# The first load of a decode kernel, cut into eight transfers of 16 rows

## The chip, the cores and the metric

The kernel runs on one core of one Trainium2 chip. Times are device microseconds (us) of that core. Executions of one kernel agree within about 0.3% (six of the kernel before: 353.45 to 353.86 us). A profile is one such execution with the hardware profiler on; its span is some 2 us shorter than the timed figure, so spans are compared with spans and times with times.

## The reference

One new token passes through two branches, mixed by a scalar gate. Branch A is attention with 32 query heads over 8 cached key/value heads of 32,768 positions; branch B is a small gated feed-forward layer. Everything is bf16. The code is shortened.

```python
def _A_ref(x, k_cache, v_cache, wq, wo):           # x [1,1,512], wq [512, 4096]
    q = (x @ wq).reshape(B, Sq, Hq, Dh).transpose(0, 2, 1, 3)
    ...
    scores = jnp.einsum("bhqd,bhkd->bhqk", q, k) * (Dh ** -0.5)
    p = _softmax(scores, axis=-1)
    o = jnp.einsum("bhqk,bhkd->bhqd", p, v)        # k, v: [1, 8, 32768, 128] each
    return o.transpose(0, 2, 1, 3).reshape(B, Sq, Hq * Dh) @ wo

def _B_ref(x, w_gate, w_up, w_down):
    return (_silu(x @ w_gate) * (x @ w_up)) @ w_down

g = _sigmoid((x * gate_w).sum(-1, keepdims=True))
return g * a + (1 - g) * b
```

The two caches are 128 MiB together and every byte is read once. The arithmetic is small; the bytes are the work.

## The kernel before

All loads are issued by the SyncE queue, in one fixed order, into a ring of five slots of 32 KB per partition. Each slot is 128 partitions (rows) high. wq comes first. The code is shortened; its comments are ours.

```python
stream = [("wq",), ("K", 0, 0), ("F1",), ("K", 0, 1), ("F2",)]     # F1: w_gate, w_up; F2: w_down
for g in range(1, G):
    for hf in range(2):
        stream += [("K", g, hf), ("V", g - 1, hf)]
stream += [("V", G - 1, 0), ("V", G - 1, 1), ("wo",)]
...
wq_v = slot_of(("wq",)).rearrange("p (c n) -> p c n", c=KC)        # 128 rows, 32 KB each
...
@block.sync
def _(sp):
    for i, e in enumerate(stream):
        ld = sem_ld[place[e]]
        if e in before:
            sp.wait_ge(*released[before[e]])       # the slot's last reader
        if e[0] == "wq":
            sp.dma_start(wq_v, A_wq.rearrange("(p c) n -> p c n", c=KC)).then_inc(ld, 16)
        ...
        elif e[0] == "F2":
            sp.dma_start(wd, B_w_down.rearrange("(p j) n -> p j n", j=FC)).then_inc(ld, 16)
...
def emit_q():                                      # TensorE
    take(load_sem(("wq",)), 16)
    for h in range(H):
        for c in range(KC):
            ins = pe.matmul(...)                   # q = x @ wq
```

Partition p of the slot gets rows 4p to 4p+3 of wq, which are 32 KB in one piece in memory. In the trace wq's 128 rows are 128 packets of 32 KB, and wq's semaphore gets sixteen updates, from 12.51 to 13.31 us. We read this as sixteen DMA engines with eight rows each, every one of which adds one to the semaphore when its share has landed, hence the wait for 16.

Of the kernel before, what the change touches and what calls it, by code (L numbers as in the profile page):

```python
# [13 lines left out]
def bass_gated_mix__gqa_block_cached__swiglu_ffn__decode_kernel(  # L14
# [23 lines left out]
    KC = D // 128  # L38
# [21 lines left out]
    NSC = 2  # L60
    NET = 2
    SCALE = float(DH) ** -0.5
    WO_CUT = (16, 8, 4, 4)
    assert NI * PB == 32 and sum(WO_CUT) == WOJ

# [19 lines left out]
    with ExitStack() as es:  # L85

        def S_(name):
            return es.enter_context(nc.semaphore(name))
# [5 lines left out]
        sem_ldv = S_("s_ldv")  # L94
        sem_ldo = [S_(f"s_ldo{i}") for i in range(len(WO_CUT))]
        sem_x = S_("s_x")
# [130 lines left out]
        def slot_of(entry):  # L227
            return ring[:, place[entry], :]

        def kv_slot(entry):  # L230
            return slot_of(entry).rearrange("p (r d) -> p r d", r=RH)

        wq_v = slot_of(("wq",)).rearrange("p (c n) -> p c n", c=KC)
# [12 lines left out]
        def load_sem(entry):  # L246
            return sem_ld[place[entry]]

        with nc.Block("main") as block:
# [60 lines left out]
# [4 lines that stand above are left out]
                    if e in before:  # L314
                        sp.wait_ge(*released[before[e]])
                    if e[0] == "wq":
                        sp.dma_start(wq_v, A_wq.rearrange("(p c) n -> p c n", c=KC)).then_inc(
                            ld, 16
                        )
                    elif e[0] == "F1":  # L320
                        sp.dma_start(wg, B_w_gate.rearrange("(p c) f -> p c f", c=KC)).then_inc(
                            ld, 16
                        )
                        sp.dma_start(wu, B_w_up.rearrange("(p c) f -> p c f", c=KC)).then_inc(
                            ld, 16
                        )
                    elif e[0] == "F2":
                        sp.dma_start(wd, B_w_down.rearrange("(p j) n -> p j n", j=FC)).then_inc(
                            ld, 16
                        )  # L330
                    elif e[0] == "wo":
                        src = A_wo.rearrange("(p j) n -> p j n", j=WOJ)
                        j0 = 0
                        for c, n in enumerate(WO_CUT):
                            sp.dma_start(wo_v[:, j0 : j0 + n, :], src[:, j0 : j0 + n, :]).then_inc(  # L335
                                sem_ldo[c], 16
                            )
                            j0 += n
                    else:
                        kind, g, hf = e  # L340
                        src = (A_k_cache if kind == "K" else A_v_cache)[
                            0, g, hf * (S // 2) : (hf + 1) * (S // 2), :
                        ].rearrange("(p r) d -> p r d", r=RH)
                        dst = kv_slot(e)
                        if e == ("V", G - 1, 1):
                            sp.dma_start(dst[:, : RH // 2, :], src[:, : RH // 2, :]).then_inc(  # L346
                                ld, 16
                            )
                            sp.dma_start(dst[:, RH // 2 :, :], src[:, RH // 2 :, :]).then_inc(  # L349
                                sem_ldv, 16  # L350
                            )
                        else:
                            sp.dma_start(dst, src).then_inc(ld, 16)  # L353
                sp.wait_ge(sem_res, 1)
                sp.dma_start(
                    out[0, 0, :].rearrange("(c n) -> c n", c=OC), res[0:128:32, :]
                ).then_inc(sem_out, 16)
                sp.wait_ge(sem_out, 16)

            @block.tensor  # L360
            def _(pe):
                def take(sem, n):
                    pe.wait_ge(sem, n)
                    pe.sem_inc(sem, -n)  # L364
# [19 lines left out]
                    ).then_inc(sem_pe_g, 1)  # L384

                def emit_q():
                    take(load_sem(("wq",)), 16)
                    for h in range(H):
                        for c in range(KC):
                            ins = pe.matmul(  # L390
                                ps_m[:, M_Q0 + h : M_Q0 + h + 1],
                                wq_v[:, c, h * DH : (h + 1) * DH],
                                xT[:, c : c + 1],
                                start=(c == 0),
                                stop=(c == KC - 1),
                            )
                    ins.then_inc(sem_pe_q, 1)
                    pe.wait_ge(sem_sel, 2)
                    pe.wait_ge(sem_qT, 1)
                    for e in range(2):  # L400
                        ins = pe.matmul(
                            ps_m[:, M_QE + e * H : M_QE + (e + 1) * H],
                            sel[:, e, :],
                            qT[:, :],
                            start=True,
                            stop=True,
                        )
                    ins.then_inc(sem_pe_qe, 1)
# [127 lines left out]
                pe.wait_ge(sem_ident, 2)  # L536
                pe.wait_ge(sem_osel, 1)
                emit_q()
                emit_k(0, first=True)
                emit_ffn()  # L540
# [33 lines left out]
                j0 = 0  # L574
                for c, n in enumerate(WO_CUT):
                    pe.wait_ge(sem_ldo[c], 16)
# [13 lines left out]
            def _(act):  # L590
# [15 lines left out]
                for g in range(G):  # L606
# [3 lines left out]
                    for hf in range(2):  # L610
                        f = 2 * g + hf
                        if f >= 2:
# [5 lines left out]
                            bias=nbias[:, 0:1],  # L618
                            scale=SCALE,
                            accum_out=esum[:, g, hf : hf + 1],  # L620
# [8 lines left out]
            def _(dve):  # L629
# [101 lines left out]
                def emit_k(hf, each):  # L731
# [10 lines left out]
                    if hf == 0:  # L742
# [12 lines left out]
                        dve.scalar_tensor_tensor(  # L755
                            gsel[:, :], gmax[:, :], -SCALE, mask4[:, :], ALU.mult, ALU.mult
                        ),
# [99 lines left out]
```

## Time and profile before

| | before |
|---|---|
| time, median of 3 (range) | 353.69 us (353.55 to 353.71) |
| span of the profiled run | 351.6 us |
| bytes read | 148.11 MB |
| load queue's packets, share of 16 engines' span | 98.3% |
| TensorE busy / VectorE busy | 72% / 56% |

The page's data-rate line has the GB/s moved in each of 40 equal slices of the span. The line of the load queue (q1) has its packets, its MB and the share of sixteen engines' span that the packets took.

```profile
GB/s 325 436 406 438 421 440 439 429 427 429 431 432 436 429 429 432 440 425 429 432 440 425 432 429 440 429 429 429 440 432 425 432 436 432 429 429 436 414 418 184
...
q1 hardware_dynamic: 5912, 148.12, 98.3%
```

From the second slice to the last but one, the rate stays within 406 to 440. The engines are full from end to end, and the first and last slices are the only thin ones.

The table of stretches has, for each stretch, its length, the busy time (and instruction count) of TensorE, weight loads, VectorE, ScalarE and GpSimd, then TensorE's granted clock, the DMA engines' share and the GB/s. A packet is counted whole in the stretch in which it starts, so short stretches are rough and a share can exceed 1.

```profile
core 0: us, PE busy (x) PEld busy (x) DVE busy (x) ACT busy (x) POOL busy (x), PEclk, DMA share, GB/s
4.00:12.00 8.00, 1.00 (x10) 0.83 (x10) 0.55 (x4) 0.17 (x1) 0.00 (x0) 1.00 0.97 410
12.00:20.00 8.00, 3.11 (x117) 3.14 (x118) 2.23 (x12) 0.00 (x0) 2.02 (x7) 1.00 1.03 442
20.00:28.00 8.00, 4.30 (x36) 4.17 (x34) 3.72 (x12) 0.30 (x1) 0.00 (x0) 1.00 0.96 401
28.00:36.00 8.00, 7.74 (x73) 5.35 (x71) 7.51 (x13) 0.00 (x0) 0.00 (x0) 1.00 1.04 449
...
44.00:100.00 56.00, 43.75 (x450) 32.49 (x449) 38.55 (x71) 5.01 (x13) 0.76 (x2) 0.90 1.01 433
```

410 GB/s while wq lands, and 433 later.

SyncE's timeline (start, duration, instruction) shows when the loads are issued:

```profile
0.73 0.38 SPq L317 DMA_DIRECT2D ring<-in_A_wq_dram  x1
1.18 0.41 SPq L353 DMA_DIRECT2D ring<-in_A_k_cache_dram  x1
...
37.12 0.33 SPq L353 DMA_DIRECT2D ring<-in_A_k_cache_dram  x1
```

One issue for wq at 0.73 us, taking 0.38 us. The six first issues are done by 3.7 us; the next waits for a free slot until 37.12 us.

TensorE's timeline has the two places where it takes up the early loads (line 390 multiplies with wq, line 446 transposes the first K). In brackets stand the idle time before and what ended it:

```profile
16.89 3.55 PE L390 MATMUL ps<-xT,ring 128*128 128x1 bf16 x128 [6.67 <-PEq L364]
...
24.36 4.58 PE L446 MATMUL ps<-ident_f,ring 128*128 128x128 f32 x24 [2.74 <-PEq L364]
```

The end of the chain of waits, in order of time (start, duration, what):

```profile
308.15 38.86 DMA ring<-in_A_wo_dram
...
349.19 0.35 DVE res L821
```

The chain hangs on the last wo transfer. From its landing (348.19 us by the semaphore records) to the end of the span are 3.4 us.

Behind these views stand the packet records of the trace file. The lines below are worked out from them and are no view of the profile. Taken sixteen at a time in order of start, the 32 KB packets (one row of wq, then of K) of the first loads read:

```
before  row 1   start 1.77 to 2.77, mean  1.98   took 1.25 to 2.11, mean 1.887   mean end  3.87
before  row 2   start 3.64 to 4.16, mean  3.87   took 1.22 to 1.24, mean 1.237   mean end  5.10
before  row 5   start 7.28 to 8.14, mean  7.59   took 1.21 to 1.70, mean 1.271   mean end  8.86
before  row 8   start 10.91 to 11.76, mean 11.29  took 1.21 to 1.23, mean 1.214   mean end 12.50
before  row 9   start 12.12 to 12.98, mean 12.50  took 1.21 to 1.21, mean 1.213   mean end 13.71
```

Rows 1 to 8 are wq, row 9 the first row of K on each engine. A row takes 1.213 us on one engine: 32,768 B / 1.213 us = 27.0 GB/s, times sixteen 432 GB/s.

### The profile page before, as it was taken

How to read it: one execution, taken by the hardware profiler on the slowest of the kernel's cores; microseconds unless marked ns; L12 is line 12 of the kernel's file. 1: busy time of each engine (PE TensorE's matmuls, PEld its weight loads, DVE VectorE, ACT ScalarE, POOL GpSimd, SP SyncE). 2: the span in 40 equal slices, each digit the busy share in tenths (PEclk: the TensorE clock that was granted, in tenths of full speed). 3: DMA queues.
4: the chain of work that ended last, by engine and by line, in shares of the span. 5: the costliest groups of instructions: out<-in, count | busy, mean ns of one | idle time of the engine just before them, and what ended most of it. 6: DMA issues, size and time to landing. Idle time of an engine off the chain costs nothing. (4 is left out here: it accounts for less than half of the span.)

```text
span 351.6 us, 6018 instructions
## 1 busy us (share of the span) xinstructions
PE 252.5 (72%) x2623; PEld 184.6 (53%) x2623; DVE 196.8 (56%) x367; ACT 17.6 (5%) x52; POOL 5.6 (2%) x22
## 2 busy tenths in 40 slices
PE   0159896978395957858495968768497929688755
PEld 0157884745282626546383838455474618475423
DVE  1329276958184845838283756648365917558211
ACT  1000001100100010000100010000100010000100
POOL 0200000000000000000000000000000000000000
PEclk9999679999789998989789698989779987969665
DMA  8999999999999999999999999999999999999994
GB/s 325 436 406 438 421 440 439 429 427 429 431 432 436 429 429 432 440 425 429 432 440 425 432 429 440 429 429 429 440 432 425 432 436 432 429 429 436 414 418 184
DMA packets 5924, 148.24 MB, mean 422 GB/s; under 512 B 666, under 2 KB 668, under 8 KB 924
## 3 DMA queue, kind: packets, MB, share of 16 engines
q1 hardware_dynamic: 5912, 148.12, 98.3%
q8 instruction: 7, 0.11, 0.1%
q14 instruction: 1, 0.01, 0.0%
q10 hardware_dynamic: 4, 0.00, 0.0%
HBM read 148.11 MB, written 0.00 MB: 421 GB/s over the span
## 5 line engine op out<-in xcount | busy, mean ns | idle before, releaser
L736 DVE COPY ktT<-ps 128x1024 bf16<-128x1024 bf16 x256 | 163.3, 685 | 95.5 <-PE ps L446 92.9
L446 PE MATMUL ps<-ident_f,ring 128*128 128x128 f32 x1024 | 158.2, 311 | 56.0 <-PEq L364 56.0
L446 PEld LDWEIGHTS ps<-ident_f,ring 128*128 128x128 f32 x1024 | 133.8, 161 | 89.8 <-issue 65.6
L460 PE MATMUL ps<-ktT,qc 128*32 128x512 bf16 x512 | 41.6, 402 | 15.2 <-DVE ktT L736 15.1
L510 PE MATMUL ps<-ring,ET 128*16 128x512 bf16 x512 | 33.6, 407 | 2.9 <-DMA ring<-in_A_v_cache_dram 2.9
L510 PEld LDWEIGHTS ps<-ring,ET 128*16 128x16 bf16 x512 | 13.3, 92 | 19.3 <-DMA ring<-in_A_v_cache_dram 3.8
L460 PEld LDWEIGHTS ps<-ktT,qc 128*32 128x32 bf16 x512 | 7.9, 95 | 28.1 <-DVE ktT L736 24.3
L741 DVE TENSOR_REDUCE pmaxf<-ps 128x1 f32<-128x512 f32 x16 | 11.1, 692 | 13.7 <-DVEq L740 13.7
L525 PEld LDWEIGHTS ps<-osel,pv_sb 128*128 128x128 f32 x72 | 11.6, 244 | 3.0 <-issue 3.0
L525 PE MATMUL ps<-osel,pv_sb 128*128 128x4 f32 x72 | 11.3, 281 | 1.8 <-PEq L364 1.8
L598 ACT ACTIVATE qc<-qz 128x112 bf16<-128x112 bf16 x8 | 2.4, 296 | 198.6 <-DVE nbias L759 186.5
L614 ACT ACTIVATE P<-ps,nbias 128x512 bf16<-128x512 f32 x16 | 10.7, 675 | 30.2 <-DVE nbias L759 30.1
L772 DVE COPY pv_sb<-ps 128x512 f32<-128x512 f32 x9 | 6.1, 682 | 6.1 <-PE ps L510 6.1
L390 PE MATMUL ps<-xT,ring 128*128 128x1 bf16 x128 | 3.6, 165 | 6.7 <-PEq L364 6.7
L306 POOL PARTITION_ALL_REDUCE gmax<-pmax x8 | 3.0, 372 | 307.4 <-DVE pmax L748 307.4
L492 PE MATMUL ps<-ident,P 128*128 128x128 bf16 x64 | 6.2, 219 | 1.9 <-ACT P L614 1.4
L766 DVE COPY ET<-ps 128x512 bf16<-128x512 bf16 x16 | 6.7, 416 | 1.3 <-PE ps L492 1.3
L415 PEld LDWEIGHTS ps<-xT,ring 128*128 128x128 bf16 x112 | 6.8, 159 | 0.4 <-issue 0.4
L390 PEld LDWEIGHTS ps<-xT,ring 128*128 128x128 bf16 x128 | 3.5, 104 | 6.7 <-issue 6.7
L415 PE MATMUL ps<-xT,ring 128*128 128x1 bf16 x112 | 6.9, 198 | 0.0
L373 PE MATMUL ps<-ones_bf,x_row 1*128 1x1 bf16 x4 | 0.3, 171 | 8.5 <-DMA gw_row<-in_gate_w_dram 8.5
L492 PEld LDWEIGHTS ps<-ident,P 128*128 128x128 bf16 x64 | 4.8, 98 | 2.8 <-ACT P L614 1.9
(71 smaller groups left out, 36.9 us busy)
## 6 DMA issues: line engine op xcount, KB each, us to landing
ring<-in_A_k_cache_dram SPq DMA_DIRECT2D x16, 4096.0 KB, 24.9
ring<-in_A_v_cache_dram SPq DMA_DIRECT2D x15, 4096.0 KB, 32.5
ring<-in_A_wq_dram SPq DMA_DIRECT2D x1, 4096.0 KB, 12.6
ring<-in_A_v_cache_dram SPq DMA_DIRECT2D x2, 2048.0 KB, 29.4
ring<-in_A_wo_dram SPq DMA_DIRECT2D x1, 2048.0 KB, 36.0
ring<-in_B_w_gate_dram SPq DMA_DIRECT2D x1, 1792.0 KB, 26.7
ring<-in_B_w_up_dram SPq DMA_DIRECT2D x1, 1792.0 KB, 30.6
ring<-in_B_w_down_dram SPq DMA_DIRECT2D x1, 1792.0 KB, 43.5
```

Of the source, the lines that this page charges most:

```text
L390: ins = pe.matmul(ps_m[:, M_Q0 + h : M_Q0 + h + 1], wq_v[:, c, h * DH : (h + 1) * DH], xT[:, c : c + 1], start=(c == 0), stop=(c == KC - 1),)
L415: ins = pe.matmul(ps_m[:, base + j : base + j + 1], wt[:, c, :].rearrange("d (p j) -> d j p", j=FC)[:, j, :], xT[:, c : c + 1], start=(c = ...
L446: ins = pe.transpose(stb[:, t * 64 : (t + 2) * 64], two.bitcast(FP32), ident_f[:, :])
L460: ins = pe.matmul(ps_sc[hf][32 * c : 32 * c + 32, :], qc[:, e, 24 - PB * i : 56 - PB * i], kt[:, e, :], start=(i == 0 and e == 0), stop=(i ...
L492: ins = pe.transpose(ps_pt[:, hf * 512 + m * 128 : hf * 512 + (m + 1) * 128], P[:, hf, m * 128 : (m + 1) * 128], ident[:, :],)
L510: ins = pe.matmul(ps_pv[32 * c : 32 * c + 2 * PB, :], ET[:, hf, col : col + 2 * PB], src[:, i0 : i0 + 2, c, 2 * m : 2 * m + 2, :].rearrang ...
L525: ins = pe.matmul(ps_m[:, M_OT : M_OT + HPG], pv_sb[:, r * DH : (r + 1) * DH], osel[:, r * HPG : (r + 1) * HPG], start=(r == 0), stop=(r = ...
L614: act.activation(P[:, hf, :], ps_sc[hf], ACT.Exp, bias=nbias[:, 0:1], scale=SCALE, accum_out=esum[:, g, hf : hf + 1],).then_inc(sem_exp, 1)
L736: dve.tensor_copy(ktT[:, q % NKT, :], pst[q % NST]).then_inc(sem_cp, 1)
L741: ins = dve.tensor_reduce(pmaxf[:, hf : hf + 1], ps_sc[hf], AX.X, ALU.max)
L766: dve.tensor_copy(ET[:, hf, :], ps_pt[:, hf * 512 : (hf + 1) * 512]).then_inc(sem_ptc, 1)
L772: dve.tensor_copy(pv_sb[:, :], ps_pv).then_inc(sem_pvc, 1)
```

## The change: intent and diff

The intent is a faster start. The sixteen first packets start over a whole microsecond (1.77 to 2.77 us). If the first transfer held only one row for each engine, each might get its first row sooner. Rows r, r+8, r+16 and so on go in transfer r.

```diff
+    WQ_CUT = 8
...
                     if e[0] == "wq":
-                        sp.dma_start(wq_v, A_wq.rearrange("(p c) n -> p c n", c=KC)).then_inc(
-                            ld, 16
-                        )
+                        src = A_wq.rearrange("(p c) n -> p c n", c=KC)
+                        for r in range(WQ_CUT):
+                            sp.dma_start(wq_v[r::WQ_CUT, :, :], src[r::WQ_CUT, :, :]).then_inc(
+                                ld, 16
+                            )
...
                 def emit_q():
-                    take(load_sem(("wq",)), 16)
+                    take(load_sem(("wq",)), 16 * WQ_CUT)
```

Same bytes, same 32 KB packets, same place in SBUF; seven more issues. No engine's order of instructions changes otherwise (line numbers move by three).

## The prediction

> **What bounds the kernel now.** The page's part 3 puts the load queue's packets at 98.3% of 16 engines' span: 148.12 MB in 351.6 us. In the packet records a 32 KB packet (one row of wq, K or V) takes 1.213 us on one engine, 27.0 GB/s, 432 for sixteen, with no gaps between packets; the table of stretches reads 431 to 433 GB/s from 30 to 300 us. PE is 72% busy, VectorE 56%. The chain of waits ends in the last wo transfer (11%) and a tail of 3 us after its landing at 348.2 us. So the time is: first packet (1.77 us), byte stream, tail. What lengthens the stream adds in full; compute that starts later costs nothing while it keeps ahead.
>
> **The start.** SyncE issues wq at 0.73 us. The sixteen first packets start between 1.77 and 2.77 us (twelve by 2.01) and take 1.7 to 2.1 us (the last 1.25). wq lands engine by engine from 12.51 to 13.31 us. TensorE takes it up at 16.86 us, since it waits for constants (GpSimd restarts at 12.4 us).
>
> **What the change removes and adds.**
> - Intended gain: each engine gets its first row at once. At best the last start moves from 2.77 to about 2.0 us: 0.8 us.
> - Issues: seven more on SyncE, about 0.47 us each with gaps, 3.3 us. They stay ahead of the engines (a row takes 1.21 us), and the loads behind them are not needed until wq is through. About 0.
> - Packets: the same; seven more completion writes per engine[...].
> - **The partitions written at once.** This decides. [...]
>
> **On the critical path.** All of it, as the stream has no slack: +9.7 us, less up to 0.8 us of start: +8.9 to +9.7. Everything later shifts with it: PE's q work (3.6 us) starts at about 22 us rather than 16.9, still ahead of the first K load (24.2 us, then about 33).
>
> **Predicted time: 362.6 us (+2.5%)**, range 353.0 to 364.0. Two humps: about two thirds at 361.5 to 363.5, a quarter at 353 to 354[...], the rest between (engines fall out of step). Chances: faster by over 2%: 0.01; within 2%: 0.32; slower by over 2%: 0.67.
>
> **What would show it.** Table of stretches, 4 to 12 us: about 216 GB/s in place of 410; first 32 KB packets 2.4 us; wq landing at about 22 us after eight issues; K's first landing at about 33 us; from 35 us on the same 432 GB/s; the same tail. Right on the start: first packets all within about 0.3 us.
>
> **What would make it wrong.** [...] Then the time stays at 353 to 358.

The sum was +9.7 us (each of the eight wq rows of an engine 1.213 us longer, 2.43 us in all), less up to 0.8 us at the start: +8.9 to +9.7 us. The 362.6 us predicted are 353.7 + 8.9. That a row would double was not shown when this was written.

## The result, and the profile after

| | before | after |
|---|---|---|
| time, median of 6 (range) | 353.62 us (353.45 to 353.86) | 364.05 us (363.80 to 364.33) |
| span of the profiled run | 351.6 us | 362.0 us |
| ratio | 1 | 1.0295 (95%: 1.0282 to 1.0308) |

The change made the kernel slower by 10.4 us, 2.95%. The prediction had said slower by 8.9 us, with a range that ends 0.05 us below the measured median.

The data rate by slices and the load queue after the change:

```profile
GB/s 174 232 290 419 448 407 433 455 409 440 422 442 427 431 438 420 449 413 453 413 438 427 442 427 427 442 420 449 413 438 424 442 427 435 435 427 442 413 412 188
...
q1 hardware_dynamic: 6024, 148.12, 98.3%
```

The three first slices fell from 325, 436 and 406 to 174, 232 and 290 GB/s; the rest is as it was. The queue's engines are still "98.3% busy": a packet that takes 2.55 us in place of 1.21 counts as busy for all of it. The share of busy engines does not see this loss; the rate does.

The table of stretches after (same columns):

```profile
4.00:12.00 8.00, 1.01 (x10) 0.84 (x10) 0.55 (x4) 0.17 (x1) 0.16 (x1) 1.00 1.00 205
12.00:20.00 8.00, 0.00 (x0) 0.00 (x0) 2.22 (x12) 0.00 (x0) 1.86 (x7) 1.00 1.21 250
20.00:28.00 8.00, 3.55 (x128) 3.50 (x128) 0.62 (x4) 0.00 (x0) 0.00 (x0) 1.00 0.84 332
28.00:36.00 8.00, 1.65 (x9) 1.60 (x10) 1.34 (x8) 0.30 (x1) 0.00 (x0) 1.00 0.93 396
...
44.00:100.00 56.00, 48.42 (x564) 35.93 (x562) 38.43 (x69) 3.38 (x8) 0.62 (x2) 0.91 1.00 429
```

205 GB/s in place of 410 while wq lands: half. From 44 us on, 429 against 433.

SyncE's timeline:

```profile
0.74 5.01 SPq L320 DMA_DIRECT2D ring<-in_A_wq_dram  x8
5.79 0.58 SPq L356 DMA_DIRECT2D ring<-in_A_k_cache_dram  x1
...
47.32 0.33 SPq L356 DMA_DIRECT2D ring<-in_A_k_cache_dram  x1
```

The eight issues take 5.01 us, 0.63 us each. The next load is issued at 5.79 us. Its data is not needed until 22 us, so the queue itself is not the cause. The issue that waits for a slot moved from 37.12 to 47.32 us, by 10.2 us.

TensorE:

```profile
23.75 3.55 PE L393 MATMUL ps<-xT,ring 128*128 128x1 bf16 x128 [16.49 <-PEq L367]
...
34.57 4.57 PE L449 MATMUL ps<-ident_f,ring 128*128 128x128 f32 x24 [6.09 <-PEq L367]
```

TensorE now does wait for wq (idle for 16.5 us before line 393), but it is through with q at 28.5 us and still waits for K until 34.57 us. That moved by 10.2 us too.

The end of the chain of waits:

```profile
318.37 38.86 DMA ring<-in_A_wo_dram
...
359.56 0.35 DVE res L824
```

The same end, 10.2 to 10.4 us later.

The packet records, again sixteen at a time:

```
after   row 1   start 2.11 to 2.83, mean  2.29   took 1.81 to 2.72, mean 2.293   mean end  4.58
after   row 2   start 4.12 to 4.95, mean  4.59   took 2.53 to 2.55, mean 2.542   mean end  7.13
after   row 5   start 11.75 to 12.59, mean 12.24  took 2.39 to 2.40, mean 2.388   mean end 14.62
after   row 8   start 19.25 to 20.09, mean 19.73  took 2.54 to 2.55, mean 2.549   mean end 22.28
after   row 9   start 21.80 to 22.64, mean 22.28  took 1.46 to 1.90, mean 1.641   mean end 23.92
after   row 10  start 23.69 to 24.09, mean 23.92  took 1.21 to 1.23, mean 1.219   mean end 25.14
```

Rows 2 to 8 take 2.39 to 2.55 us in place of about 1.21, on all sixteen engines. The first K row (row 9) takes 1.64 us, and from row 10 on it is 1.22 us again. Row 5, the one with r = 4, is the short one, with 2.39 us. Where the 10 us come from, by mean ends: the start 0.31 us later (1.98 to 2.29), row 1 longer by 0.41, rows 2 to 8 by 9.07 (17.70 against 8.63), row 9 by 0.43; together 10.2. Nothing of it is given back: the mean landing of the first K moved by 10.24 us (22.76 to 33.00), that of the last wo transfer by 10.25 (347.27 to 357.52).

### The profile page after: what moved, and what is told of

The parts are those of the page before. It is cut to its first block, busy times and chain, and to the rows that moved or that the text cites. A ratio compares the mean times of both kernels' runs of the same rounds, so it can differ in the third digit from the quotient of the medians.

```text
span 362.0 us, 6025 instructions
## 1 busy us (share of the span) xinstructions
PE 252.3 (70%) x2623; PEld 184.6 (51%) x2623; DVE 196.6 (54%) x367; ACT 17.6 (5%) x52; POOL 5.6 (2%) x22
## 3 DMA queue, kind: packets, MB, share of 16 engines
q1 hardware_dynamic: 6024, 148.12, 98.3%
## 5 line engine op out<-in xcount | busy, mean ns | idle before, releaser
L393 PE MATMUL ps<-xT,ring 128*128 128x1 bf16 x128 | 3.6, 165 | 16.5 <-PEq L367 16.5
L393 PEld LDWEIGHTS ps<-xT,ring 128*128 128x128 bf16 x128 | 3.5, 104 | 16.5 <-issue 16.5
```

What stands on the lines that cost most here:

```text
L393: ins = pe.matmul(ps_m[:, M_Q0 + h : M_Q0 + h + 1], wq_v[:, c, h * DH : (h + 1) * DH], xT[:, c : c + 1], start=(c == 0), stop=(c == KC - 1),)
```

## The experiments

Three theories were set against each other.

- **T1, the partitions.** How long a row takes depends on which SBUF partitions a transfer writes.
- **T2, colliding reads.** Sixteen engines read wq at a pitch of 256 KB at the same moment, and collide in memory.
- **T3, a cost per transfer.** Every transfer ends with a completion on each engine (so we read the load queue's rise from 5,912 to 6,024 packets, by 7 × 16 of 4 B); if the next row waited for it, eight transfers at 1.33 us extra (2.55 − 1.21) would give the same 10.6 us.

All three fit the result. Diffs below are against the changed kernel, unless noted. Each run was timed in three rounds beside the kernel before, on the same chip. E1 to E4, E5 to E8 and E9 to E10 shared chips; "before" measured 353.77, 353.66 and 353.85 us there.

| run | wq goes as | row 2 took | time | ratio (95%) |
|---|---|---|---|---|
| before | 1 × 128 rows | 1.24 us | 353.62 | 1 |
| after | 8 × 16, step 8 | 2.54 us | 364.05 | 1.0295 (1.0282 to 1.0308) |
| E1 | 8 × 16, step 8; reads consecutive | 2.55 us | 363.54 | 1.0278 (1.0261 to 1.0295) |
| E2 | 8 × 16 consecutive | 4.61 us | 379.84 | 1.0738 (1.0720 to 1.0756) |
| E3 | 8 × 128 rows, an eighth of the columns | (4 KB packets) | 354.00 | 1.0001 (0.9984 to 1.0018) |
| E4 | 1 × 128; w_down as 8 × 16, step 8 | 1.23 us | 359.13 | 1.0146 (1.0129 to 1.0163) |
| E5 | 7 × 16, step 7, then 16 consecutive | 2.13 us | 363.09 | 1.0268 (1.0251 to 1.0285) |
| E6 | 4 × 32, step 4 | 1.24 us | 353.73 | 1.0006 (0.9989 to 1.0023) |
| E7 | 2 × 64, step 2 | 1.24 us | 353.80 | 1.0005 (0.9988 to 1.0022) |
| E8 | as after | 2.53 us | 363.73 | 1.0282 (1.0265 to 1.0299) |
| E9 | 4 × 32 consecutive | 2.56 us | 363.61 | 1.0279 (1.0262 to 1.0296) |
| E10 | 2 × 64 consecutive | 2.54 us | 363.84 | 1.0288 (1.0270 to 1.0305) |

"Row 2 took" is the mean of the second sixteen 32 KB packets.

### E1: the writes as in the change, the reads consecutive

```diff
-                            sp.dma_start(wq_v[r::WQ_CUT, :, :], src[r::WQ_CUT, :, :]).then_inc(
-                                ld, 16
-                            )
+                            sp.dma_start(
+                                wq_v[r::WQ_CUT, :, :], src[16 * r : 16 * r + 16, :, :]
+                            ).then_inc(ld, 16)
```

> Eight transfers of 16 rows into every eighth partition, as in the change, but each read from 16 consecutive rows of wq (wrong result on purpose). T1[...], so rows of about 2.55 us, wq through at about 22.3 us, time 353.6 + 10.4 = 364 (362.5 to 365). T2, the reads at a pitch of 256 KB collide in HBM: pitch is now 32 KB, rows back to about 1.21 us, time 353 to 355. T3, each transfer's completion holds its engine up by about 1.3 us: eight transfers as before, 364.

The rows of wq land in the wrong partitions, on purpose. (The check of the result passed all the same, so it says nothing about the order of these rows.) Measured: 363.54 us, rows of 2.55 us. The table of stretches:

```profile
4.00:12.00 8.00, 1.01 (x10) 0.84 (x10) 0.55 (x4) 0.17 (x1) 0.69 (x3) 1.00 1.10 225
12.00:20.00 8.00, 0.00 (x0) 0.00 (x0) 2.23 (x12) 0.00 (x0) 1.34 (x5) 1.00 1.13 234
```

225 GB/s against 205 after the change in this stretch (and 234 against 250 in the next): the same rate over both. T2 falls: it is not the order of the reads. (The ratio is 1.0278 against 1.0295; the intervals overlap, and a small part for the reads can be neither claimed nor excluded.)

### E2: sixteen consecutive rows

```diff
-                            sp.dma_start(wq_v[r::WQ_CUT, :, :], src[r::WQ_CUT, :, :]).then_inc(
-                                ld, 16
-                            )
+                            sp.dma_start(
+                                wq_v[16 * r : 16 * r + 16, :, :], src[16 * r : 16 * r + 16, :, :]
+                            ).then_inc(ld, 16)
```

> Eight transfers of 16 consecutive rows into 16 consecutive partitions (right result). T1: [...]first rows 4.9 to 5.1 us, later rows between 2.5 and 5 us[...]; wq through between 33 and 42 us, time +20 to +29, 374 to 383. T2: source pitch 32 KB, so 353 to 355. T3: still eight transfers, 364.

Measured: 379.84 us, +26.1. The table of stretches:

```profile
4.00:12.00 8.00, 1.00 (x10) 0.84 (x10) 0.55 (x4) 0.17 (x1) 0.83 (x4) 1.00 1.16 131
```

131 GB/s with eight transfers as before, and reads as plain as they can be. T3 and T2 had 364 and 354. Rows 2 to 8 all take 4.60 to 4.64 us, 3.8 times the 1.213 us of the kernel before. They did not become shorter, as the expectation had allowed for (2.5 to 5 us); the engines stay in step. (The 131 GB/s of the stretch are rough at 4.6 us a packet; the packet records give 16 × 32,768 B / 4.62 us = 113.5 GB/s.)

### E3: eight transfers, all partitions

```diff
-                            sp.dma_start(wq_v[r::WQ_CUT, :, :], src[r::WQ_CUT, :, :]).then_inc(
-                                ld, 16
-                            )
+                            c, n = r // 2, r % 2 * 2048
+                            sp.dma_start(
+                                wq_v[:, c, n : n + 2048], src[:, c, n : n + 2048]
+                            ).then_inc(ld, 16)
```

> Eight transfers of all 128 partitions and an eighth of the columns each, 4 KB a row (right result). T1: [...]only smaller packets, 159 ns for 4 KB (as measured in w_down) against 152 for an eighth of 1.213 us, 64 of them per engine: +0.5, time 353.5 to 354.8. T2: source order as in the kernel before, about 0. T3: eight completions per engine, 8 x 1.33 = +10.6, time 364.

Measured: 354.00 us, ratio 1.0001. The table of stretches:

```profile
4.00:12.00 8.00, 1.00 (x10) 0.83 (x10) 0.55 (x4) 0.17 (x1) 0.31 (x2) 1.00 1.02 405
```

Eight transfers, eight completions and seven more issues cost nothing that the times show (the first K lands 0.28 us later in the mean). T3 falls. It is also the change's intent without its partitions, and here it gains nothing. (The 159 ns in the expectation are the median of wo's 4 KB packets in the kernel before; w_down, which it names, has packets of 14 KB.)

### E4: the same cut elsewhere, in smaller rows

The diff is against the kernel before; wq stays whole.

```diff
-                        sp.dma_start(wd, B_w_down.rearrange("(p j) n -> p j n", j=FC)).then_inc(
-                            ld, 16
-                        )
+                        src = B_w_down.rearrange("(p j) n -> p j n", j=FC)
+                        for r in range(8):
+                            sp.dma_start(wd[r::8, :, :], src[r::8, :, :]).then_inc(ld, 16)
...
-                    take(load_sem(("F2",)), 16)
+                    take(load_sem(("F2",)), 16 * 8)
```

> wq whole as before; the w_down load, in the middle of the stream, is cut into eight transfers of every eighth row instead, 14 KB a row (right result). T1: a row of 0.535 us should take 2.1 x that, 1.12 us: 8 x 0.59 = +4.7, time 358.3 (357.5 to 359.2), and PE, which uses w_down some 10 us after its landing, waits for nothing more. T2: pitch 112 KB, no power of two, about 0 (353.5 to 354.5). T3: a fixed 1.33 us per transfer, +10.6, time 364.

Measured: 359.13 us. By the ratio, 1.46% of 353.77 is +5.2 us. The table of stretches, first the kernel before:

```profile
40.00:44.00 4.00, 4.00 (x70) 4.00 (x69) 0.00 (x0) 0.00 (x0) 0.00 (x0) 0.50 0.95 408
44.00:48.00 4.00, 4.00 (x22) 4.00 (x21) 2.54 (x6) 0.18 (x1) 0.00 (x0) 0.50 1.10 464
48.00:52.00 4.00, 4.00 (x39) 2.71 (x37) 3.48 (x7) 0.00 (x0) 0.00 (x0) 0.94 1.03 442
```

then E4:

```profile
40.00:44.00 4.00, 3.77 (x63) 3.69 (x62) 0.00 (x0) 0.18 (x1) 0.00 (x0) 0.61 1.01 204
44.00:48.00 4.00, 2.58 (x12) 2.61 (x13) 1.29 (x2) 0.00 (x0) 0.00 (x0) 0.50 1.08 249
48.00:52.00 4.00, 4.00 (x27) 3.05 (x26) 3.01 (x7) 0.00 (x0) 0.00 (x0) 0.61 0.94 219
52.00:56.00 4.00, 4.00 (x38) 2.99 (x35) 3.73 (x7) 0.00 (x0) 0.00 (x0) 1.00 0.99 414
```

The rate halves where w_down lands, 40 to 52 us, and only there. w_down's 14 KB packets took 1.04 us in the mean against 0.536. So the loss goes with the bytes, not with the number of transfers (eight here too, and half the loss), and it is not a matter of the start of the kernel. In this stretch the engines were less in step (single packets from 0.54 to 1.76 us, nine in ten of them from 0.69 to 1.29), and the K rows in flight beside the first w_down rows were slowed too: K(0,1) landed 0.74 us later in the mean, its last share at 45.29 us in place of 42.38. TensorE waited 1.65 us before it took up that K, which the expectation had not foreseen.

### E5: a step of 7

```diff
-                        for r in range(WQ_CUT):
-                            sp.dma_start(wq_v[r::WQ_CUT, :, :], src[r::WQ_CUT, :, :]).then_inc(
-                                ld, 16
-                            )
+                        for r in range(WQ_CUT - 1):
+                            sp.dma_start(wq_v[r:112:7, :, :], src[r:112:7, :, :]).then_inc(ld, 16)
+                        sp.dma_start(wq_v[112:128, :, :], src[112:128, :, :]).then_inc(ld, 16)
```

> Seven transfers of 16 rows at a step of 7 partitions (r, r+7, ... r+105), then one of rows 112 to 127; wq is complete, the result right. T1: [...]of the first sixteen packets about 12 take what the first packets of the kernel before took (1.3 to 2.1 us) and 4 take 2.3 us or more; rows 2 to 7 are about 1.21 us for most engines and 2.55 for some; only the last transfer[...] is slow, 3.5 to 5.7 us. [...]+5 to +7 for the last engine, time 358 to 361. T3 (fixed cost per transfer) and any cost of striding as such: all sixteen packets alike, 2.55 us, 364.

Measured: 363.09 us, and here the expectation failed. The table of stretches:

```profile
4.00:12.00 8.00, 1.00 (x10) 0.84 (x10) 0.55 (x4) 0.17 (x1) 1.33 (x5) 1.00 1.09 295
12.00:20.00 8.00, 0.00 (x0) 0.00 (x0) 2.23 (x12) 0.00 (x0) 0.69 (x3) 1.00 1.08 197
```

T1's expectation had 1.21 us for most engines and 2.55 us for some in rows 2 to 7. They did not come so. Mean durations of rows 2 to 8 are 2.13, 2.14, 1.81, 1.63, 1.97, 2.23 and 3.71 us, and row 2 lies between 1.91 and 2.20 us for all sixteen: all are slowed, not some. (Neighbouring transfers overlap here by 0.7 to 1.7 us, so the rows of two transfers run side by side, and no run takes it apart. But no packet of row 2 took less than 1.91 us.) What slows all sixteen is not shown. It stays open.

### E6 and E7: larger transfers at a smaller step

The comment in the diff is ours.

```diff
-    WQ_CUT = 8
+    WQ_CUT = 4          # E7: WQ_CUT = 2
```

> Four transfers of 32 rows (every fourth row), two rows per engine. [...] T1 with rows dealt out in order:[...] rows 2.4 to 2.55 us, +9 to +10.5, 362.6 to 364.3. T1 with engines chosen by partition[...], rows 1.21 us, 353.4 to 354.5. T3: 4 x 1.33 = +5.3, 359.

> Two transfers of 64 rows (every second row), four rows per engine. T1 with rows dealt out in order:[...] rows 2.4 to 2.55 us, +9 to +10.5, 362.6 to 364.3. T1 with engines chosen by partition: 353.4 to 354.5. T3: 2 x 1.33 = +2.7, 356.4.

Measured: 353.73 and 353.80 us, ratios 1.0006 and 1.0005. E6's table of stretches:

```profile
4.00:12.00 8.00, 1.01 (x10) 0.84 (x10) 0.55 (x4) 0.17 (x1) 0.06 (x1) 1.00 1.06 451
```

Rows of 1.24 us (row 2), as in the kernel before. Of T1's two forecasts the one with rows dealt out in order (2.4 to 2.55 us) fails, and the other (1.21 us, 353.4 to 354.5) holds. Which engine took which row the records do not tell; they carry no engine and no address.

### E8: the changed kernel again

> The changed kernel once more, as the yardstick on the chip of these runs: 363.5 to 364.5 under every theory; rows of 2.55 us.

Measured: 363.73 us, ratio 1.0282, rows of 2.53 us. The result repeats on another chip.

### E9 and E10: larger transfers of consecutive rows

The comment in the diff is ours.

```diff
-                            sp.dma_start(wq_v[r::WQ_CUT, :, :], src[r::WQ_CUT, :, :]).then_inc(
-                                ld, 16
-                            )
+                            sp.dma_start(
+                                wq_v[32 * r : 32 * (r + 1), :, :],
+                                src[32 * r : 32 * (r + 1), :, :],
+                            ).then_inc(ld, 16)          # WQ_CUT = 4; E10: 64 rows, WQ_CUT = 2
```

> Four transfers of 32 consecutive rows into 32 consecutive partitions, two rows per engine. It tells apart why 32 rows at a step of 4 cost nothing. N, only transfers with a single row per engine are slow, whatever they write: 353.4 to 354.5, as with the step of 4. T1[...], so rows of 2.4 us or more: about 2.5 us and +10 (364) if rows are dealt to engines in order[...], about 4.6 us and +20 to +27 (374 to 381) if they are dealt as in the 128-row transfer, scaled down. If each engine is chosen by the partition[...]: +1 to +3 (355 to 357).

> Two transfers of 64 consecutive rows into 64 consecutive partitions, four rows per engine[...]. N: 353.4 to 354.5. T1: about +10 (364) dealt in order, +20 to +27 (374 to 381) dealt as in the 128-row transfer, scaled down. Engine chosen by the partition: +0 to +3.

Measured: 363.61 and 363.84 us. The table of stretches of E9 (E10 reads 209 GB/s in the first of them):

```profile
4.00:12.00 8.00, 1.01 (x10) 0.84 (x10) 0.55 (x4) 0.17 (x1) 0.37 (x2) 1.00 1.07 221
```

Two transfers of 64 consecutive rows lose as much as eight of 16. The pairs E6 and E9, and E7 and E10, have the same number of transfers, rows per engine and bytes, and differ in which partitions a transfer writes (and in the order of the reads, which E1 excludes). With a step, over all 128 partitions, the time is 354 us (353.73 and 353.80), with a block of consecutive partitions 364 (363.61 and 363.84). That is the cleanest of the runs, and it settles that the partitions decide, against any rule of "small transfers" or "one row per engine".

What each pattern of a transfer gave, by row 2: 64 consecutive rows 2.54 us (E10), 32 consecutive 2.56 (E9), 16 consecutive 4.61 (E2); 64 rows at a step of 2 and 32 at a step of 4, 1.24 us (E7, E6); 16 at a step of 8, 2.54 (the change). Why these sets of partitions differ no run shows.

One thing does not fit. E9 and E10 came out where the expectations put "dealt in order", which E6 and E7 had ruled out. Dealt like the 128-row transfer, scaled down, E9 was expected to have rows of about 4.6 us; its rows 2 to 4 took 2.54 to 2.57. So neither way of dealing named here fits all runs, and how rows are dealt to engines, in the 128-row transfer too, stays open.

## Why the prediction was right or wrong

The direction was right, and so were half the rate (205 GB/s against 410) and that all of it is on the critical path. That the partitions decide is shown by E1 to E3, E9 and E10. The time was 364.05 us against 362.6 predicted and a range that ended at 364.0; the repeat (E8) gave 363.73. The forecast of +8.9 us was short by 1.3 to 1.5. The step that failed is the sum "+9.7 us, less up to 0.8 us of start": the slowed row was sized too small (2.43 us; most took 2.55), the gain of 0.8 us at the start did not come, and the first K row, 0.43 us longer, was missing. The stream was shifted by 10.2 us in place of 8.9.

- **"What bounds the kernel": right.** The stream of bytes has no slack. 10.24 us lost at the first K are 10.25 us at the last wo.
- **The slowed row, 2 × 1.213 = 2.43 us in the forecast: mis-sized.** Rows 2 to 8 took 17.70 us where they had taken 8.63: +9.07 against 7 × 1.213 = 8.49 predicted, +0.58. Most of them took 2.55 us, 2.10 times the 1.213 us of before, where the forecast had taken twice. Why it is more than twice no run shows.
- **"At best the last start moves from 2.77 to about 2.0 us": wrong.** The first packets started between 2.11 and 2.83 us, in the mean 0.31 us later than before. Start and first row together cost 0.72 us; the prediction had them at 1.21 − 0.8 = 0.41. Why they start later is not settled: over the runs their mean start lies between 1.88 us (E2) and 2.39 us (E8), and neither the number of transfers nor the step orders them (E10, two consecutive blocks, has 2.38, E9, four of them, 1.93).
- **The first K row: not foreseen.** Row 9 took 1.64 us in place of 1.21, +0.43, although it belongs to a transfer of 128 rows. The engines reach it at different times, from 21.80 to 22.64 us, so the first of them write K while the last still write wq. That this slows row 9 is a reading; no run isolates it. Row 5 differs from its neighbours too, 2.39 us in place of 2.55, and so it does in E1, E8, E9 and E10 (2.39 to 2.42); why is not shown.
- **Packets and issues: right.** Seven more issues and completions cost nothing that E3 can show (1.0001, with an interval of 0.6 us to either side).
- **"PE's q work starts at about 22 us, still ahead of the first K": right in kind** (23.75 us, 1.75 later than said; K at 34.57).
- **The signs: mostly right.** 205 GB/s from 4 to 12 us (216 predicted), wq's landing from 22.8 to 23.5 us (22), K's first landing at 32.65 to 34.43 us (33), the same rate after, about the same tail (3.4 us before, 3.5 after).
- **The escape to 353 to 358 us did not happen.** The engines stayed slow to the last row of wq (2.55 us in row 8), and were not limited by themselves (they took 1.21 us a row in other transfers). The sign "first packets all within about 0.3 us" did not appear either: they started over 0.72 us. E6 and E7 show that transfers of 32 rows at a step of 4, or 64 at a step of 2, are not slowed (rows of 1.24 us).

The three terms, +0.58, +0.31 and +0.43, add up to 1.3 us: 8.9 + 1.3 = 10.2, the shift of the stream.

## What to carry to other kernels

Judge a cut of a load by the partitions that each piece writes, not by the number of pieces: pieces over columns (E3: 1.0001), or 32 or 64 rows at a step of 4 or 2 over all 128 partitions (E6, E7: 1.0006, 1.0005), were free here. 16 rows at a step of 8, and 32 or 64 consecutive rows, halved the rate for as long as they ran (205, 221 and 209 GB/s from 4 to 12 us against 410), and 16 consecutive rows cut it to about a quarter (E2: 113.5 GB/s against 432). "One row for each DMA engine" is not balance in itself: the change's rows took 2.54 us where they had taken 1.24 (row 2). When a stream of loads fills the DMA engines from end to end, look at GB/s by stretch and at the duration of one packet, because a slowed packet counts as busy: 98.3% of the span before and after.
